# Chunked attention with memory keys, then a sine-activated two-layer network: x in two tiles, and the front of the first batch in another order

## The chip, the cores and the metric

The kernel runs on one core of one Trainium2 chip. A core has TensorE (PE) for matrix products, with its weight loads shown apart (PEld), VectorE (DVE), ScalarE (ACT), GpSimd (POOL) and SyncE (SP), and 16 DMA engines. POOL and SP have queues from which DMAs are issued. The metric is the device time of one execution, in microseconds.

## The reference

There are 4 batches of 768 tokens with 8 heads of 64. Tokens attend in chunks of 32: each chunk to 16 tokens before it, itself, 8 after it, and 8 memory keys of the batch and head. The result, as 3072 rows of 512, goes through two layers of width 2048 with a sine activation.

```python
for c in range(nc):                      # 24 chunks of 32 tokens
    q_c = q[:, :, c_start:c_end]
    k_full = np.concatenate([mem_k, k[:, :, l_start:r_end]], axis=2)
    v_full = np.concatenate([mem_v, v[:, :, l_start:r_end]], axis=2)
    a = softmax(q_c @ k_full.T / sqrt(64))
    out[:, :, c_start:c_end] = a @ v_full
x = out.transpose(0, 2, 1, 3).reshape(3072, 512)
h = x @ w_in
s = np.sin(alpha * h)
g = h + s * s / alpha
return g @ w_out
```

## The kernel before

**Stages.** The four batches go one after the other. For each there is attention, which leaves x transposed in a tile `xT` (128 partitions x 4 groups of features `kt` x 768 tokens, bf16), then the first layer (`layer`, lines 692 to 712): 16 blocks `ft` of 128 hidden features, for each of which `first` runs four matmuls over `kt` for each half of 384 tokens (`half_first`, line 508), then a sine on ACT (line 518), a square on ACT, DVE or POOL as a letter of the string `squares` says (lines 544 and 547), and a combination on DVE, `snake` (line 551), which writes the bf16 tile `gT`. The second layer (`second`, line 566 is its matmul) is a generator that `feed.take(n)` runs n matmuls of; a finished piece of 128 rows is copied out of PSUM by `end_o` (line 579 on DVE, line 581 on ACT) and sent by SP. So the second layer of one batch runs in pieces between the attention steps of the next batch and between its blocks.

**Order.** The program is scheduled by hand: each engine works in the order in which the code issues, and waits only for the data and the buffers of an instruction. The eight PSUM banks are handed out from rings (`plan`, `take_bank`); a ring is a written list, and a bank comes free when its last reader is done. `two` takes a bank and the one behind it, `single` one of the banks 6 and 7.

**Batch 0.** `attention_first` (line 390) works by pairs of heads `hp` and by halves of the tokens. `turn_k`, `turn_q` transpose keys and queries on PE; `sc_half` makes scores (lines 341 and 349 on PE) and exponentials (line 356 on ACT); `pv` makes the values (line 368 on PE, lines 374 and 375 on DVE); `x` transposes one block on PE (line 385) and copies it to `xT` (line 388, on ACT unless told otherwise). `warm(n)` issues n matmuls on zeros (line 336) into the bank at the head of the ring of `single`. In before the order from the third `pv` unit on is (1,0), (1,1), (2,0), (2,1), (3,0), (3,1). After the block (3,0), `ahead(0)` runs the first token half of layer block 0, and after (3,1) `ahead(1)` that of block 1; each has its sine and its square on ACT.

**Loads.** POOL issues the loads: keys and queries of batch 0 by pairs, v of batch 0 in parts (heads 0 and 1, then 2 and 3, 4 and 5, 6 and 7; each in two copies for two ranges of partitions), w_in in five, w_out in two, then memory values, keys and queries of batch 1, and the memory keys of batches 2 and 3 in two copies (line 685). The timeline of POOL shows the later of these waiting for the landing of earlier ones. POOL's squares of the first layer are behind them in its program.

**Later batches.** `attention` (line 473) works by 8 steps of 96 tokens. The first five blocks of x are transposed by SP's DMA transpose (line 492), the last three by PE and a DVE copy (line 329). `shares` says how many second-layer matmuls go into each step. Near the end, `ahead(0)`, `ahead(1)` and `ahead(2)` run the first token halves of three layer blocks. While `state["attending"]` holds, `end_o` copies on DVE.

Of the kernel before, what the change touches and what calls it, by code (L numbers as in the profile page):

```python
# [9 lines left out]
P = 128  # L10
QW = 96
# [31 lines left out]
def kernel(  # L43
# [76 lines left out]
    memk_st = consts.tile([P, 2, H * D], BF, name="memk_st")  # L120
# [17 lines left out]
    def load_rows(b):  # L138
        for jt in order:
# [18 lines left out]
            kst[64:72], memk_st[64:72, b - 2, :].unsqueeze(1).to_broadcast([NM, NJ, H * D])  # L158
# [117 lines left out]
    state = {"n": 0, "attending": False}  # L276
# [45 lines left out]

    def turn_x(xT, j, x_blk):
# [5 lines left out]
        nc.vector.tensor_copy(xT[:, :, QW * j:QW * j + QW], xtp)  # L329
# [52 lines left out]
    def unit_turn(xT, hp, half, x_blk, copy):  # L382
# [5 lines left out]
        copy(xT[:, hp, HALF * half:HALF * half + HALF].rearrange("p (j c) -> p j c", j=4), xtp)  # L388

    def attention_first(kq, alphas, ahead):  # L390
        xT = xp.tile([P, KT, S], BF, name="xT")
# [60 lines left out]
        pv(1, 1)  # L452
        sc_half(3, 1)
        x(1, 0)
        pv(2, 0)
        warm(1)
        x(1, 1)
        pv(2, 1)
        warm(2)
        x(2, 0)  # L460
        pv(3, 0)
        warm(2)
        x(2, 1)
        pv(3, 1)
        warm(1)
        x(3, 0)
        nc.scalar.preload_act_table(ACTF.Sin)
        ahead(0, 0, xT)
        x(3, 1, nc.vector.tensor_copy)
        ahead(1, 0, xT)  # L470
        return xT

    def attention(b, stream, shares, lag, crossed, beside=iter(()), beside_from=0):
        xT = xp.tile([P, KT, S], BF, name="xT")
        ptl, xbl = {}, {}
        state["attending"] = True
        for s in range(NJ + lag + 1):
# [8 lines left out]
            j = s - lag  # L486
            if j == NJ:
                ahead(1, 0, xT)
            if 0 <= j < NJ:
                xbl[j] = values(b, j, ptl.pop(j))  # L490
                if j < crossed:
                    nc.sync.dma_start_transpose(
                        xT[:, :, QW * j:QW * j + QW], xbl.pop(j)[:].rearrange("p g e d -> p (g e d)")
                    )
            stream.take(n - n // 2)
            if j == NJ - 1:
                ahead(0, 0, xT)
            if crossed <= j - 1 < NJ:
                turn_x(xT, j - 1, xbl.pop(j - 1))
        ahead(2, 0, xT)  # L500
        state["attending"] = False
# [4 lines left out]
    def half_first(hT, ft, hf, xT):  # L506
        for kt in range(KT):
            nc.tensor.matmul(  # L508
                hT[:, hf, 0:HALF],
                w_in_sb[:, kt, P * ft:P * ft + P],  # L510
                xT[:, kt, HALF * hf:HALF * hf + HALF],
# [5 lines left out]
    def sine(u, hT, ft, e):  # L517
        nc.scalar.activation(u[:, e], hT[:, e, 0:HALF], ACTF.Sin, scale=alpha_sb[:, ft:ft + 1])  # L518

    def ahead(ft, hf, xT):  # L520
        if ft < 3:
            hT = two("big")
            half_first(hT, ft, hf, xT)
            u = mlp.tile([P, 2, HALF], F32, name="u", bufs=4)
            e = slice(hf, hf + 1)
            sine(u, hT, ft, e)
            nc.scalar.activation(u[:, e], u[:, e], ACTF.Square)
            begun[ft] = (hT, u)

    def first(ft, xT, square, started=None):  # L530
        e = slice(0, 2)
# [280 lines left out]
```

## Time and profile before

| | us |
|---|---|
| median of 4 runs | 219.99 |
| lowest and highest of them | 218.99, 220.24 |
| the profiled execution | 219.91 |
| its span, first to last instruction | 218.1 |
| PE busy in it | 210.2 (96%) |
| ACT busy | 153.1 (70%) |
| DVE busy | 137.5 (63%) |
| POOL busy | 82.1 (38%) |

A row of the timeline gives the start in us from the first instruction, the length, the engine, the line, the operation, what is written from what, the shapes and the number of instructions that the row joins; in brackets stand the idle time of the engine before it and what ended that. A busy PE is not PE at its peak, since the ends of matmuls are modelled; what counts is the distance from start to start. The chain of waits follows the last instruction back to the first. A row of the busy times by stage gives the stage, its length, and for each engine the busy time and the number of instructions, then the granted TensorE clock and the DMA engines' share and rate. A row of the DMA issues gives the size of one and the time from issue to landing.

### The profile page before, as it was taken

Reading aid. Unit: us, or ns where it says so; the run is one execution under the profiler, and the core shown is the slowest. Engines: PE = TensorE matmul, PEld = TensorE weight load, DVE = VectorE, ACT = ScalarE, POOL = GpSimd, SP = SyncE. Lnnn points to the kernel's source line nnn. Section 1 sums busy time; section 2 is a strip of 40 time slices with the busy share of each in tenths; the row PEclk is TensorE's granted clock in tenths of the full one; section 3 lists DMA queues with packets and bytes.
Section 4 is the critical chain, followed back from the end, with each engine's and each line's share of the span. In section 5 each row is a group of like instructions: output and inputs, shape, how many; then the busy total and the mean of one; then the engine's idle time right before and its main releaser. Section 6 shows DMA issues by size and latency. Waiting matters only on the chain.

```text
span 218.1 us, 4457 instructions
## 1 busy us (share of the span) xinstructions
PE 210.2 (96%) x1687; PEld 114.2 (52%) x1687; DVE 137.5 (63%) x246; ACT 153.1 (70%) x238; POOL 82.1 (38%) x102
## 2 busy tenths in 40 slices
PE   7999998999999999999999999999999999999993
PEld 2555664555545555544555555545555555544453
DVE  5866659884527889995775766575854753871110
ACT  2457797895778899998967777988776778651010
POOL 7996663598700599500078099100000000000000
PEclk9999999999999999999999999999999999999999
DMA  5999999999999599999449999995330110111212
GB/s 76 160 171 168 206 209 206 200 193 122 112 193 187 56 155 147 164 165 124 99 62 174 112 111 150 191 218 150 68 103 2 48 51 2 48 48 51 96 48 96
DMA packets 98877, 26.96 MB, mean 124 GB/s; under 512 B 86808, under 2 KB 95912, under 8 KB 98856
## 3 DMA queue, kind: packets, MB, share of 16 engines
q0 software_dynamic: 71520, 14.82, 92.5%
q1 hardware_dynamic: 27336, 11.86, 26.3%
q8 instruction: 13, 0.21, 0.4%
q14 instruction: 8, 0.07, 0.1%
HBM read 29.69 MB, written 6.29 MB: 165 GB/s over the span
## 4 chain that ended last, share of the span: by engine, by line
PE 73%; DMA 10%; POOL 5%; DVE 5%; ACT 3%; issue 3%; DVEq 0%; ACTq 0%; POOLq 0%
PE ps L566 35%; PE ps L508 30%; DMA w_in_sb<-in_moe_w_in_dram 5%; DMA vw<-in_v_dram 4%; PE ps L283 3%; PE ps L309 2%; ACT u L518 2%; DVE gT L551 2%; DMA xT<-x_blk 2%; PE ps L589 2%; POOL vw L183 1%; POOL u L547 1%; POOL q_bf L172 1%; POOL k_bf L172 1%; PE ps L244 1%
## 5 line engine op out<-in xcount | busy, mean ns | idle before, releaser
L566 PE MATMUL ps<-w_out_sb,gT 128*128 128x512 bf16 x368 | 95.5, 380 | 0.2
L508 PE MATMUL ps<-xT,w_in_sb 128*128 128x384 bf16 x512 | 90.8, 326 | 1.9 <-DMA xT<-x_blk 0.8
L551 DVE SCALAR_TENSOR_TENSOR gT<-u,inv_alpha,ps 128x768 bf16<-128x768 f32 (+1 forms) x75 | 65.7, 895 | 23.4 <-ACT u L544 16.2
L518 ACT ACTIVATE u<-ps,alpha_sb 128x768 f32<-128x768 f32 (+1 forms) x75 | 59.4, 801 | 20.7 <-PE ps L508 20.1
L508 PEld LDWEIGHTS <-w_in_sb 128*128 128x128 bf16 x512 | 49.6, 98 | 39.0 <-issue 3.5
L566 PEld LDWEIGHTS <-gT 128*128 128x128 bf16 x368 | 32.8, 98 | 29.1 <-issue 0.5
L544 ACT ACTIVATE u<-u 128x768 f32<-128x768 f32 (+1 forms) x40 | 31.5, 787 | 1.2
L296 ACT ACTIVATE pt<-ps,biasm 128x256 bf16<-128x256 f32 x72 | 28.7, 472 | 4.6 <-PE ps L283 1.8
L579 DVE COPY o_sb<-ps 128x512 f32<-128x512 f32 x17 | 11.7, 689 | 27.3 <-PE ps L566 27.2
L183 POOL DMA_DIRECT2D vw<-in_v_dram x15 | 18.2, 1219 | 0.3 <-issue 0.3
L547 DVE TENSOR_TENSOR u<-u 128x768 f32<-128x768 f32 (+1 forms) x18 | 16.0, 886 | 1.7 <-ACT u L518 1.6
L316 DVE TENSOR_TENSOR x_blk<-ps,rinv 96x512 bf16<-96x512 f32 x24 | 16.5, 687 | 0.8
L143 POOL DMA_DIRECT2D kst<-in_k_dram x16 | 11.1, 694 | 5.8 <-DMA vw<-in_v_dram 5.2
L262 ACT COPY kT<-ps 128x672 bf16<-128x672 bf16 x8 | 5.7, 718 | 9.7 <-PE ps L247 7.3
L581 ACT COPY o_sb<-ps 128x512 f32<-128x512 f32 x6 | 3.5, 584 | 12.7 <-PE ps L566 12.7
L148 POOL DMA_DIRECT2D kst<-in_k_dram x16 | 11.7, 728 | 0.3 <-issue 0.2
L336 PE MATMUL ps<-idle 128*128 128x512 bf16 x30 | 10.4, 459 | 1.3 <-DVE vw L628 1.2
L309 PEld LDWEIGHTS <-pt 128*128 128x128 bf16 x192 | 9.0, 98 | 4.1
L153 POOL DMA_DIRECT2D qst<-in_q_dram x12 | 10.8, 901 | 1.0 <-DMA vw<-in_v_dram 1.0
L547 POOL TENSOR_TENSOR u<-u 128x768 f32<-128x768 f32 (+1 forms) x6 | 8.3, 1396 | 5.9 <-ACT u L518 5.9
L283 PEld LDWEIGHTS <-kT 64*128 64x128 bf16 x192 | 4.9, 94 | 10.4 <-issue 9.9
L315 DVE RECIPROCAL rinv<-ps 96x8 f32<-96x8 f32 x24 | 4.8, 202 | 8.2 <-ACT pt L296 5.2
(83 smaller groups left out, 146.0 us busy)
## 6 DMA issues: line engine op xcount, KB each, us to landing
out_dram<-o_sb SPq DMA_DIRECT2D x23, 256.0 KB
w_out_sb<-in_moe_w_out_dram POOLq DMA_DIRECT2D x2, 1024.0 KB, 18.0
w_in_sb<-in_moe_w_in_dram POOLq DMA_DIRECT2D x3, 512.0 KB, 10.5
vw<-in_v_dram POOLq DMA_DIRECT2D x3, 512.0 KB, 9.1
qst<-in_q_dram POOLq DMA_DIRECT2D x12, 128.0 KB, 5.9
vw<-in_v_dram POOLq DMA_DIRECT2D x2, 448.0 KB, 12.6
kst<-in_k_dram POOLq DMA_DIRECT2D x14, 64.0 KB, 5.6
kst<-in_k_dram POOLq DMA_DIRECT2D x14, 56.0 KB, 5.3
```

What stands on the lines that cost most here:

```text
L148: nc.gpsimd.dma_start(kst[72:72 + n, j, :].rearrange("p (h d) -> p h d", d=D), k[b, :, QW * j + 48:QW * j + 48 + n, :].rearrange("h p d -> ...
L183: nc.gpsimd.dma_start(vw[p0:p1, c0:c1, 0:D], flat[r0:r0 + QW * (c1 - c0)].rearrange("(n t) d -> t n d", t=QW)[0:p1 - p0],)
L296: nc.scalar.activation(pt[:, 0:H * QW].rearrange("p (g e c) -> p g e c", g=2, e=4)[:, :, :, 32 * m:32 * m + 32], sc[:, :, 0:4 * QW].rearra ...
L309: nc.tensor.matmul(otv[:, e, hp, :], pt[:, QW * i:QW * i + P], vws[b % 2][:, 2 * hp + e, j, 0:D + 1],)
L316: nc.vector.tensor_tensor(out=x_blk[:].rearrange("p g e d -> p e g d"), in0=otv[0:QW, :, :, 0:D], in1=rinv[:].unsqueeze(3).to_broadcast([Q ...
L508: nc.tensor.matmul(hT[:, hf, 0:HALF], w_in_sb[:, kt, P * ft:P * ft + P], xT[:, kt, HALF * hf:HALF * hf + HALF], start=(kt == 0), stop=(kt ...
L518: nc.scalar.activation(u[:, e], hT[:, e, 0:HALF], ACTF.Sin, scale=alpha_sb[:, ft:ft + 1])
L544: nc.scalar.activation(u[:, e], u[:, e], ACTF.Square)
L547: eng.tensor_tensor(out=u[:, e], in0=u[:, e], in1=u[:, e], op=ALU.mult)
L551: nc.vector.scalar_tensor_tensor(out=gT[:, ft, :].rearrange("p (e c) -> p e c", e=2)[:, e], in0=u[:, e], scalar=inv_alpha[:, ft:ft + 1], i ...
L566: nc.tensor.matmul(ps[:, bank, :], gT[:, ft, P * s:P * s + P], w_out_sb[:, ft, :], start=(ft == 0), stop=(ft == FT - 1),)
L579: nc.vector.tensor_copy(o_sb[:], ps[:, bank, :])
```

## The change

`xT` becomes a list of two tiles, one for each half of the tokens; `alloc_x` makes them and `block_of` finds the place of a block of 96. In `attention_first` the first halves of pairs 2 and 3 go before the second halves of pairs 1 to 3; two fewer fillers are issued after the third unit; three layer blocks instead of two have their first token half in the front, placed between the second-half blocks, with banks that are named; their sines come at the end, and their squares go to POOL, DVE and POOL instead of ACT. The loads of w_out, memory values, keys and queries of batch 1 (`next_loads`) are issued within the front. The two loads of memory keys are gone: `load_rows` sends the rows from `memk_bf`, which the front fills for all batches. The letters of batch 0's squares and the ring of its layer are new. In batch 1's attention the last second-layer matmul comes one step earlier, and from the step on that makes the values of the last block, `end_o` copies on ACT (`state["copying"]`). The sines of `ahead` move to `half_sine`, which in later batches follows at once, as before.

```diff
--- before.py
+++ after.py
@@ -117,7 +117,6 @@
     memv_st = consts.tile([P, B, H, D], BF, name="memv_st")
     kst = consts.tile([P, NJ, H * D], BF, name="kst")
     qst = consts.tile([P, NSUB, H * D], BF, name="qst")
-    memk_st = consts.tile([P, 2, H * D], BF, name="memk_st")
     memkT = consts.tile([P, HP, 32], BF, name="memkT")
     w_in_sb = consts.tile([P, KT, d_ff], BF, name="w_in_sb")
     w_out_sb = consts.tile([P, FT, d_model], BF, name="w_out_sb")
@@ -155,7 +154,9 @@
                     q[b, :, P * t:P * t + P, :].rearrange("h p d -> p h d"),
                 )
         nc.sync.dma_start(
-            kst[64:72], memk_st[64:72, b - 2, :].unsqueeze(1).to_broadcast([NM, NJ, H * D])
+            kst[64:72],
+            memk_bf[NM * b:NM * b + NM].rearrange("n h d -> n (h d)").unsqueeze(1)
+            .to_broadcast([NM, NJ, H * D]),
         )
 
     def cross_steps(b):
@@ -273,7 +274,7 @@
 
 
 
-    state = {"n": 0, "attending": False}
+    state = {"n": 0, "attending": False, "copying": False}
 
     def scores(b, j, kind="big"):
         pitch = 104 if b < 2 else P
@@ -320,13 +321,20 @@
         )
         return x_blk
 
+    def alloc_x():
+        return [xp.tile([P, KT, HALF], BF, name=f"xT{hf}") for hf in range(2)]
+
+    def block_of(xT, j):
+        c = QW * (j % 4)
+        return xT[j // 4][:, :, c:c + QW]
+
     def turn_x(xT, j, x_blk):
         xtp = packed(single(), KT, QW)
         for kt in range(KT):
             nc.tensor.transpose(
                 xtp[:, kt, :], x_blk[:, kt].rearrange("p e d -> p (e d)"), ident[0:QW, 0:QW]
             )
-        nc.vector.tensor_copy(xT[:, :, QW * j:QW * j + QW], xtp)
+        nc.vector.tensor_copy(block_of(xT, j), xtp)
 
 
 
@@ -385,10 +393,10 @@
             nc.tensor.transpose(
                 xtp[:, jj, :], x_blk[:, jj].rearrange("p e d -> p (e d)"), ident[0:QW, 0:QW]
             )
-        copy(xT[:, hp, HALF * half:HALF * half + HALF].rearrange("p (j c) -> p j c", j=4), xtp)
-
-    def attention_first(kq, alphas, ahead):
-        xT = xp.tile([P, KT, S], BF, name="xT")
+        copy(xT[half][:, hp, :].rearrange("p (j c) -> p j c", j=4), xtp)
+
+    def attention_first(kq, alphas, ahead, next_loads):
+        xT = alloc_x()
         pt, xb = {}, {}
 
         def turn_k(hp):
@@ -449,29 +457,34 @@
         plan(big=(4, 0, 2))
         pv(1, 0)
         sc_half(3, 0)
-        pv(1, 1)
+        pv(2, 0)
         sc_half(3, 1)
         x(1, 0)
-        pv(2, 0)
         warm(1)
-        x(1, 1)
-        pv(2, 1)
+        pv(3, 0)
+        x(2, 0)
+        warm(1)
+        pv(1, 1)
+        next_loads()
         warm(2)
-        x(2, 0)
-        pv(3, 0)
-        warm(2)
-        x(2, 1)
-        pv(3, 1)
-        warm(1)
         x(3, 0)
         nc.scalar.preload_act_table(ACTF.Sin)
-        ahead(0, 0, xT)
+        plan(big=(0, 2))
+        pv(2, 1)
+        ahead(0, xT, (4, 1))
+        x(1, 1)
+        pv(3, 1)
+        ahead(1, xT, (5, 2))
+        x(2, 1)
+        ahead(2, xT, (0, 3))
+        plan(big=(4, 0, 2))
         x(3, 1, nc.vector.tensor_copy)
-        ahead(1, 0, xT)
+        for ft in range(3):
+            half_sine(ft, "PVP"[ft])
         return xT
 
     def attention(b, stream, shares, lag, crossed, beside=iter(()), beside_from=0):
-        xT = xp.tile([P, KT, S], BF, name="xT")
+        xT = alloc_x()
         ptl, xbl = {}, {}
         state["attending"] = True
         for s in range(NJ + lag + 1):
@@ -484,73 +497,88 @@
             if s >= beside_from:
                 next(beside, None)
             j = s - lag
+            state["copying"] = j >= NJ - 1
             if j == NJ:
-                ahead(1, 0, xT)
+                ahead(1, xT)
+                half_sine(1)
             if 0 <= j < NJ:
                 xbl[j] = values(b, j, ptl.pop(j))
                 if j < crossed:
                     nc.sync.dma_start_transpose(
-                        xT[:, :, QW * j:QW * j + QW], xbl.pop(j)[:].rearrange("p g e d -> p (g e d)")
+                        block_of(xT, j), xbl.pop(j)[:].rearrange("p g e d -> p (g e d)")
                     )
             stream.take(n - n // 2)
             if j == NJ - 1:
-                ahead(0, 0, xT)
+                ahead(0, xT)
+                half_sine(0)
             if crossed <= j - 1 < NJ:
                 turn_x(xT, j - 1, xbl.pop(j - 1))
-        ahead(2, 0, xT)
-        state["attending"] = False
+        ahead(2, xT)
+        half_sine(2)
+        state["attending"] = state["copying"] = False
         return xT
 
 
 
-    def half_first(hT, ft, hf, xT):
+    def half_first(bank, ft, hf, xT):
         for kt in range(KT):
             nc.tensor.matmul(
-                hT[:, hf, 0:HALF],
+                ps[:, bank, 0:HALF],
                 w_in_sb[:, kt, P * ft:P * ft + P],
-                xT[:, kt, HALF * hf:HALF * hf + HALF],
+                xT[hf][:, kt, :],
                 start=(kt == 0), stop=(kt == KT - 1),
             )
 
     begun = {}
 
     def sine(u, hT, ft, e):
-        nc.scalar.activation(u[:, e], hT[:, e, 0:HALF], ACTF.Sin, scale=alpha_sb[:, ft:ft + 1])
-
-    def ahead(ft, hf, xT):
-        if ft < 3:
-            hT = two("big")
-            half_first(hT, ft, hf, xT)
-            u = mlp.tile([P, 2, HALF], F32, name="u", bufs=4)
-            e = slice(hf, hf + 1)
-            sine(u, hT, ft, e)
-            nc.scalar.activation(u[:, e], u[:, e], ACTF.Square)
-            begun[ft] = (hT, u)
+        nc.scalar.activation(u[:, e], hT, ACTF.Sin, scale=alpha_sb[:, ft:ft + 1])
+
+    def ahead(ft, xT, banks=None):
+        if banks is None:
+            bank = take_bank("big")
+            banks = (bank, bank + 1)
+        half_first(banks[0], ft, 0, xT)
+        begun[ft] = (banks, mlp.tile([P, 2, HALF], F32, name="u", bufs=4))
+
+    def square_on(kind, x):
+        if kind == "A":
+            nc.scalar.activation(x, x, ACTF.Square)
+        else:
+            eng = nc.vector if kind == "V" else nc.gpsimd
+            eng.tensor_tensor(out=x, in0=x, in1=x, op=ALU.mult)
+
+    def half_sine(ft, square="A"):
+        banks, u = begun[ft]
+        e = slice(0, 1)
+        sine(u, ps[:, banks[0]:banks[0] + 1, 0:HALF], ft, e)
+        square_on(square, u[:, e])
+
+    def half_snake(gT, ft):
+        banks, u = begun[ft]
+        snake(gT, ft, ps[:, banks[0]:banks[0] + 1, 0:HALF], u, slice(0, 1))
 
     def first(ft, xT, square, started=None):
-        e = slice(0, 2)
         if started is not None:
-            hT, u = started
+            (_, bank), u = started
             e = slice(1, 2)
         else:
-            hT = two("h")
-            half_first(hT, ft, 0, xT)
+            bank = take_bank("h")
+            half_first(bank, ft, 0, xT)
             u = mlp.tile([P, 2, HALF], F32, name="u", bufs=4)
-        half_first(hT, ft, 1, xT)
+            e = slice(0, 2)
+        half_first(bank + (started is None), ft, 1, xT)
+        hT = ps[:, bank:bank + (2 if started is None else 1), 0:HALF]
         sine(u, hT, ft, e)
 
         def squared():
-            if square == "A":
-                nc.scalar.activation(u[:, e], u[:, e], ACTF.Square)
-            else:
-                eng = nc.vector if square == "V" else nc.gpsimd
-                eng.tensor_tensor(out=u[:, e], in0=u[:, e], in1=u[:, e], op=ALU.mult)
+            square_on(square, u[:, e])
         return hT, u, e, squared
 
     def snake(gT, ft, hT, u, e):
         nc.vector.scalar_tensor_tensor(
             out=gT[:, ft, :].rearrange("p (e c) -> p e c", e=2)[:, e],
-            in0=u[:, e], scalar=inv_alpha[:, ft:ft + 1], in1=hT[:, e, 0:HALF],
+            in0=u[:, e], scalar=inv_alpha[:, ft:ft + 1], in1=hT,
             op0=ALU.mult, op1=ALU.add,
         )
 
@@ -575,7 +603,7 @@
             rings["one"].remove(bank)
             rings["one"].append(bank)
             o_sb = mlp.tile([P, d_model], F32, name="o_sb", bufs=2)
-            if s % 2 == 0 or state["attending"]:
+            if (s % 2 == 0 or state["attending"]) and not state["copying"]:
                 nc.vector.tensor_copy(o_sb[:], ps[:, bank, :])
             else:
                 nc.scalar.copy(o_sb[:], ps[:, bank, :])
@@ -673,17 +701,17 @@
         nc.vector.tensor_copy(alpha_sb[:], at)
         nc.vector.reciprocal(inv_alpha[:], alpha_sb[:])
 
+    def next_loads():
+        for c in range(2):
+            load_w_out(c)
+        nc.gpsimd.dma_start(memv_st[64:72, 1:B].rearrange("n b h d -> n (b h) d"),
+                            mem_v[1:B].rearrange("b h n d -> n (b h) d"))
+        kq1.extend(alloc_qk())
+        load_qk(1, kq1, 0, H)
+
     feed = Feed()
-    xT = attention_first(kq, alphas, ahead)
-    for c in range(2):
-        load_w_out(c)
-    nc.gpsimd.dma_start(memv_st[64:72, 1:B].rearrange("n b h d -> n (b h) d"),
-                        mem_v[1:B].rearrange("b h n d -> n (b h) d"))
-    kq1 = alloc_qk()
-    load_qk(1, kq1, 0, H)
-    for bb in range(2):
-        nc.gpsimd.dma_start(memk_st[64:72].rearrange("n b (h d) -> n b h d", d=D)[:, bb],
-                            mem_k[2 + bb].rearrange("h n d -> n h d"))
+    kq1 = []
+    xT = attention_first(kq, alphas, ahead, next_loads)
 
 
 
@@ -694,7 +722,7 @@
         pend = []
         fed = 0
         for ft in sorted(begun):
-            snake(gT, ft, *begun[ft], slice(0, 1))
+            half_snake(gT, ft)
         for ft in range(FT):
             begin(ft)
             square = squares[ft % len(squares)]
@@ -714,8 +742,8 @@
     prs = []
 
     def begin_0(ft):
-        if ft == 2:
-            plan(h=[rings["big"][0], 6] + rings["big"][1:])
+        if ft == 3:
+            plan(h=[6] + rings["big"])
         if ft == 12:
             load_v(1)
             send_memv(1)
@@ -723,7 +751,7 @@
         if ft == 15:
             prs.extend(pair_up(kq1[n // HP], n % HP) for n in range(4))
 
-    layer(0, xT, "VPPAPAVPAVPPAAAA", begin_0, 0)
+    layer(0, xT, "PPPAVPPAAVPAAAAA", begin_0, 0)
     last4 = rings["h"]
     plan(one=(last4[0], last4[0] + 1), t=(last4[1], last4[1] + 1), big=last4[1:])
     put_memk(1)
@@ -742,7 +770,7 @@
     nc.scalar.preload_act_table(ACTF.Exp)
     load_v(2)
     feed.take(4)
-    xT = attention(1, feed, (6, 8, 4, 4, 4, 3, 3, 3, 3, 1, 1), 2, 5)
+    xT = attention(1, feed, (6, 8, 4, 4, 4, 3, 3, 3, 3, 2), 2, 5)
 
     for i in range(1, B):
         last = i == B - 1
@@ -750,13 +778,13 @@
 
         def begin(ft, i=i):
             if i == 1 and ft == 0:
-                nc.gpsimd.tensor_copy(gate[:], xT[0:1, 0, QW * 6 - 1:QW * 6])
+                nc.gpsimd.tensor_copy(gate[:], block_of(xT, 5)[0:1, 0, QW - 1:QW])
                 load_rows(2)
                 for _ in crossings:
                     pass
             if i == 2:
                 if ft == 0:
-                    nc.gpsimd.tensor_copy(gate[:], xT[0:1, 0, QW * 6 - 1:QW * 6])
+                    nc.gpsimd.tensor_copy(gate[:], block_of(xT, 5)[0:1, 0, QW - 1:QW])
                     load_v(3)
                     load_rows(3)
                 if ft >= 1:
```

## The prediction

> **What bounds the kernel now.** I read the page's parts 1 and 5 first, then the busy time by stage, then the front on PE, POOL and the DMA issues, then the places where PE is idle later.
>
> ```profile
> PE 210.2 (96%) x1687; PEld 114.2 (52%) x1687; DVE 137.5 (63%) x246; ACT 153.1 (70%) x238; POOL 82.1 (38%) x102
> L508 PE MATMUL ps<-xT,w_in_sb 128*128 128x384 bf16 x512 | 90.8, 326 | 1.9 <-DMA xT<-x_blk 0.8
> 25.60:47.10 21.50, 20.71 (x129) 12.28 (x128) 16.17 (x20) 19.12 (x25) 12.29 (x11) 1.00 1.28 205
> 75.80:96.40 20.60, 20.52 (x122) 11.79 (x121) 18.98 (x24) 19.87 (x28) 13.92 (x19) 1.00 2.04 157
> ```
>
> The windows' columns are PE, PEld, DVE, ACT, POOL. PE sets the time: only PE idleness or PE filler can be won. In the two stages of pure first-layer work (batch 0, then batch 1) ACT and DVE are at 19 to 20 of 20.6 to 21.5 us as well, so a PE that arrives earlier there soon waits for them.
>
> ```profile
> 18.97 0.40 PE L368 MATMUL ps<-vw,pt_first 128*128 128x65 bf16 x8 [0.25 <-DMA vw<-in_v_dram]
> 21.26 0.41 PE L368 MATMUL ps<-vw,pt_first 128*128 128x65 bf16 x8
> 23.02 0.41 PE L368 MATMUL ps<-vw,pt_first 128*128 128x65 bf16 x8
> 24.53 0.34 PE L385 MATMUL ps<-ident,x_blk 96*128 96x96 bf16 x4
> 24.71 1.05 PE L508 MATMUL ps<-xT,w_in_sb 128*128 128x384 bf16 x4
> 25.77 7.32 PE L508 MATMUL ps<-xT,w_in_sb 128*128 128x384 bf16 x44
> 33.87 13.39 PE L508 MATMUL ps<-xT,w_in_sb 128*128 128x384 bf16 x80 [0.79 <-DVE gT L551]
> ...
> vw<-in_v_dram POOLq DMA_DIRECT2D x1, 112.0 KB, 7.9
> vw<-in_v_dram POOLq DMA_DIRECT2D x1, 112.0 KB, 7.5
> ...
> 29.92 0.58 POOL L685 DMA_DIRECT2D memk_st<-in_mem_k_dram  x1 [1.97 <-DMA w_in_sb<-in_moe_w_in_dram]
> 30.51 2.26 POOL L547 TENSOR_TENSOR u<-u 128x384 f32<-128x384 f32 x2
> ```
>
> The L368 rows are the values of pairs 1, 2 and 3, first halves; L508 is the first layer. From 25.77 PE runs at full rate (44 matmuls, 0.163 us from start to start) until a bank waits at 33.08 for an L551 (the snake), which waits for a POOL square, which waits behind the memory-key loads: POOL stood 1.97 us for a free place in its queue. The two vw lines are DMA issues in windows around 13.5 and 15.3: second parts of v for heads 4, 5 (issued 13.17) and 6, 7 (issued 14.85). They land at 13.17 + 7.9 = 21.05 and 14.85 + 7.5 = 22.38.
>
> ```profile
> 74.77 0.69 DVE L579 COPY o_sb<-ps 128x512 f32<-128x512 f32 x1 [0.51 <-PE ps L566]
> 75.78 19.24 PE L508 MATMUL ps<-xT,w_in_sb 128*128 128x384 bf16 x116 [0.22 <-DVE xT L329]
> 154.50 3.88 DMA xT<-x_blk
> 158.51 0.81 PE L508 MATMUL ps<-xT,w_in_sb 128*128 128x384 bf16 x4 [0.82 <-DMA xT<-x_blk]
> ```
>
> Two later PE waits touch the change: batch 1's last x copy queued behind an output copy on DVE, and batch 3's wait for an x transpose.
>
> **The two x tiles: nothing.** At 24.71 the half layer starts before the last first-half x copy on ACT (24.91 to 25.39) and before any copy of x(3,1), so waits already go by region. In batch 3 the chain says that PE waited for the transpose issued at 154.50, the fourth. The fifth, the first of the second half, is issued from 157.48 to 158.70, after PE had started. The fourth is needed with two tiles too: that wait stays. Its bounds: 0.8 gained if its timing shifts by luck, nothing lost; I take 0.
>
> **The new order of the front.** Gaps measured in before: values to reciprocal 0.44, reciprocal to block ready 0.93, scores to exponential 0.80, turning to its ACT copy 0.38. On PE: values 0.25, half scores 0.70, turning 0.17, filler 0.215, half layer 0.65.
> - values(2,0) moves from 21.26 to 19.91, but its v lands at 21.05: PE idles to 21.17 (values(1,0), too, went about 0.1 after its landing). Queued behind it: half scores (3,1), 21.42, whose exponential ends at 23.0 instead of 22.0, and on ACT behind that the copy of x(1,0), to about 23.4.
> - values(3,0) goes at 22.5, right at its landing. The second filler writes the bank of x(1,0) and waits for that copy: 23.46, another 0.5 idle. values(1,1) 23.67, two fillers, x(3,0) at 24.35 (before 24.53).
> - ahead(0) 24.77 to 25.42, then x(1,1), values(3,1), ahead(1), x(2,1), ahead(2), x(3,1) without a pause, 0.17 + 0.25 + 0.65 + 0.17 + 0.65 + 0.17 = 2.07, to 27.49. The DVE copy of x(3,1) ends at 28.11, and the 16th layer matmul at 28.33.
> - next_loads moves ahead of ten pieces of the front. On POOL its five issues (w_out twice, memory values, k, q; 21.32 to 26.04) pass nothing, since POOL has no other work in the front, and each waits for a place in the queue as before: landings unchanged, 0. SP issues nothing there. The two key issues that went behind them (1.17 us, with 1.31 and 1.97 of waiting) are gone.
>
> 16 matmuls at 28.33 equal full rate from 28.33 - 16 x 0.163 = 25.73. Before, 4 at 25.77 equal 25.12. Two fillers fewer and one more half layer in the front thus end as a loss of 0.6, because v is late. ACT, too, starts its sines later, 27.4 against 26.70: two x copies stand behind the table load.
>
> **Batch 0's layer.** From 25.12, 128 matmuls at 0.1626 would end at 45.93; they end at 47.10, so waits cost 1.17, of which the one at 33 is 0.95 (start to start 1.11 instead of 0.16). Without the key loads POOL is free at 26.04, not 30.50. I replayed the layer engine by engine with the durations above, snake 0.97 (half 0.55), sine 0.93 (0.58), square on ACT 0.75, DVE 0.95 (0.55), POOL 1.47 (0.84); for before it gives 47.02. With the new squares and bank order no bank is late up to ft 12; at ft 13 one is late by 0.24 (ft 9's square on DVE). It ends at 46.76, or 46.54 without that wait: a gain of 0.26 to 0.56, I take 0.35. A rule speaks against the moved squares: the Trainium skill, GPSIMD Engine Reference, 4.1 Engine selection, puts two-input elementwise work on VectorE, GpSimd being about twice as slow. The trace has 839 ns against 551 (half), 1466 against 951: 1.5 times. By the rule the five halves that POOL now takes first are 5.5 us instead of 4.2, the square of ft 2 comes 1.3 later, and PE waits 0.8 at ft 6: the gain is gone. I take the row.
> What comes next covers the rest: ACT ends its squares at 49.9 either way and is idle 2.0 before the k copies; q lands 26.1 after its issue, at 51.25, and its first use is at 52.04, so 0.35 of earlier PE is covered, 1 us would not be. v of batch 1 (used from 63.7) is issued some 1.7 us earlier.
>
> **Batch 1.** The last output piece moves ahead of the half layer: it fills a 0.15 wait before 72.88. Its copy goes to ACT (0.58) where ACT idles 0.76; the last x copy is no longer late: 0.39 (start to start 0.55 at 75.23). So PE is 0.54 earlier. But the sines begin no earlier (73.8 against 73.73), the bank of ft 0 is free at 78.8 and PE wants it at 78.5: 0.34 goes back. Net 0.15; ends 0 and 0.54. In batches 2 and 3 an output copy of 0.58 on ACT delays the sines by about 0.4; the bank it delays was free 0.67 early in batch 2 (snake to 116.64, PE at 117.31) and 1.3 in batch 3 (164.68, 166.00): 0. If that cover were gone, 0.4 each.
> **Memory keys by SP from memk_bf:** the same issue on SP (0.72 at 75.92), from a tile filled at 5.6: 0.
>
> Sum: 219.91 (the profiled execution: span 218.1 and 1.8 around it; 0.08 below the median of 219.99) - 0.35 - 0.15 = 219.4.
>
> **The rivals.** (A, 0.50) The sum, 218.7 to 220.2. (B, 0.26) Faster: the filler's wait or the v landing costs less, layer 1 keeps all of the 0.54, and batch 3's transpose comes in time: 0.56 + 0.54 + 0.8 = 1.9, 218.0. For it: each is a real PE wait of before. Against: ACT and DVE are nearly full in both layers. (C, 0.24) Slower: the front now leaves PE 1.8 us idle between 19.9 and 23.5, with two fillers fewer, and the array falls to its half rate. The first ten fillers of before step 0.427 us, later ones 0.216: a slow state of about 4 us. PE has no slack from 23.5 to 28.3, so about 2 us: 219.4 + 2.0 = 221.4. It decides from the step after 21.2: 0.427 or 0.216. Against it: after the 0.79 idle at 33 the steps stay at 0.163, with PEclk 1.00. The Trainium skill, TensorE: Matmul & The Clock Gate, Part 1, asks an idle window of some 3.4 us; my pause is broken up by scores and values. No row here has such a mixture, so it keeps a chance. (D) That the two tiles do nothing is already in the sum.
>
> **How the numbers follow.** 0.5% is 1.1 us, about what a measurement of this kernel can tell from no change. Of A a quarter lies beyond it (0.12): faster 0.12 + 0.26 = 0.38, same 0.38, slower 0.24. The range goes from B to C: 217.9 to 221.3; A's own is 218.7 to 220.2.
>
> **What would show it.** Right: a PE wait of about 1.2 on v before the values of pair 2; the last x copy of the front at 28, not 26; sines from 27.4; no wait on L551 near 33; L508 of batch 0 ending near 46.7; no L329 wait before batch 1's layer, but one on L551 early in it; the 0.8 transpose wait still in batch 3. Wrong: L508 of batch 0 ending before 46 or after 47.3, half-rate steps in the front, or the transpose wait gone.

## The result, and the profile after

The kernel with the change took 218.95 us in the median (44 runs, 217.85 to 220.24), the kernel before 219.82 us (63 runs, 218.57 to 221.22): ratio 0.9964, 95% interval 0.9952 to 0.9976. By the ratio that is 0.79 us less, between 0.53 and 1.06 (0.87 between the two medians), inside the likeliest case of the prediction and a little faster than its 219.4.

The profiled execution of after has the same span as that of before, 218.1 us (219.86 us in all). It shows no gain because its first loads landed later: values(1,0), the start of the part that was changed, runs at 19.60, in before at 18.97. So the two traces are compared from that point on, and a time in after is to be read as 0.63 us less when it is set beside one in before.

The lines of the page, then of the busy times by stage, that answer to those shown of before (columns of the latter PE, PEld, DVE, ACT, POOL, granted clock, DMA); the stages here are the unbroken runs of first-layer matmuls, 116 of them in batch 0 against 124 in before's window, so their lengths can't be compared:

```profile
PE 210.3 (96%) x1685; PEld 114.3 (52%) x1685; DVE 136.3 (63%) x244; ACT 154.1 (71%) x241; POOL 81.2 (37%) x102
L525 PE MATMUL ps<-xT,w_in_sb 128*128 128x384 bf16 x512 | 90.8, 326 | 1.1 <-DMA xT<-x_blk 0.8
```

```profile
27.70:46.90 19.20, 19.10 (x120) 11.33 (x118) 16.25 (x21) 17.21 (x24) 12.33 (x11) 1.00 1.28 204
74.60:94.50 19.90, 19.77 (x123) 11.68 (x121) 18.00 (x24) 19.55 (x28) 15.16 (x20) 1.00 1.85 151
```

L525 is the first layer's matmul (L508 before). Its idle time fell from 1.9 to 1.1 us, and of what is left 0.8 is the transpose wait of batch 3, which the change doesn't touch. PE is now busy in 19.10 of 19.20 us of batch 0's layer.

The timeline of the front, for PE, then ACT, DVE and POOL (L376 values, L344 fillers, L535 sines, L396 the copy of a turned block, L549 squares):

```profile
19.60 0.40 PE L376 MATMUL ps<-vw,pt_first 128*128 128x65 bf16 x8 [0.21 <-DMA vw<-in_v_dram]
...
21.40 0.40 PE L376 MATMUL ps<-vw,pt_first 128*128 128x65 bf16 x8 [0.80 <-DMA vw<-in_v_dram]
...
23.67 0.38 PE L344 MATMUL ps<-idle 128*128 128x512 bf16 x1 [0.23 <-ACT xT L396]
...
24.98 0.81 PE L525 MATMUL ps<-xT,w_in_sb 128*128 128x384 bf16 x4
...
27.69 19.43 PE L525 MATMUL ps<-xT,w_in_sb 128*128 128x384 bf16 x116
46.96 0.59 PE L594 MATMUL ps<-w_out_sb,gT 128*128 128x512 bf16 x2
...
27.47 1.54 ACT L535 ACTIVATE u<-ps,alpha_sb 128x384 f32<-128x384 f32 x3
27.96 0.36 DVE L396 COPY xT<-ps 128x384 bf16<-128x384 bf16 x1 [0.77 <-PE ps L393]
28.15 4.28 POOL L549 TENSOR_TENSOR u<-u 128x384 f32<-128x384 f32 x5 [2.19 <-ACT u L535]
```

The wait for v that the prediction put at 1.2 us is there with 0.80, and the second filler behind it waits 0.23 for a copy. Then one row of 116 matmuls runs to the second layer: where before had a row of 44, a hole of 0.79 and a row of 80, after has no hole of that size. From start to start it has two short waits, 0.19 ahead of the matmul at 28.37, whose x the DVE copy of x(3,1) ends at 28.32, and 0.23 ahead of the one at 43.06, for a bank. POOL's five half squares start as soon as the first sine is done; in before POOL was still busy with the memory-key loads until 30.5.

Batch 1 and batch 2, on PE and ACT (L609 is the output copy on ACT, L334 the turning of the last blocks of x):

```profile
73.00 0.59 ACT L609 COPY o_sb<-ps 128x512 f32<-128x512 f32 x1 [0.18 <-PE ps L594]
73.76 0.58 ACT L535 ACTIVATE u<-ps,alpha_sb 128x384 f32<-128x384 f32 x1 [0.17 <-PE ps L525]
...
74.56 19.98 PE L525 MATMUL ps<-xT,w_in_sb 128*128 128x384 bf16 x120
...
111.90 0.57 ACT L609 COPY o_sb<-ps 128x512 f32<-128x512 f32 x1
111.91 0.59 PE L594 MATMUL ps<-w_out_sb,gT 128*128 128x512 bf16 x2
112.52 0.33 PE L334 MATMUL ps<-ident,x_blk 96*128 96x96 bf16 x4
```

In batch 1 the output copy fits on ACT ahead of the first sine, and PE enters the layer without the wait for DVE. In batch 2 two L594 matmuls start at 111.91 and step 0.216 us; L334 could follow at 112.34, and follows at 112.52, just after ACT's output copy (111.90 to 112.47) gives back the bank that it writes. That is a loss of 0.18 us that the prediction didn't have.

The chain of waits in batch 3, and the row at its end:

```profile
154.10 4.02 DMA xT<-x_blk
158.12 0.14 issue
158.25 0.81 PE ps L525 x4
```

```profile
158.25 0.81 PE L525 MATMUL ps<-xT,w_in_sb 128*128 128x384 bf16 x4 [0.84 <-DMA xT<-x_blk]
```

PE waits 0.84 us for the fourth transpose, as in before (0.82).

Start to start, from values(1,0) on (us; #n is the n-th first-layer matmul counted from 0, #16, #127 and so on):

| stretch | before | after | gain |
|---|---|---|---|
| values(1,0) to #16: front | 8.76 | 8.93 | -0.17 |
| #16 to #127: rest of batch 0's layer | 19.21 | 18.27 | 0.94 |
| #127 to #128: batch 1's attention | 25.94 | 26.11 | -0.17 |
| #128 to #255: batch 1's layer | 21.81 | 21.30 | 0.51 |
| #255 to #383 | 46.92 | 47.12 | -0.20 |
| #383 to #511 | 51.27 | 51.48 | -0.21 |

The sum is 0.70, close to the 0.79 of the timing. Each row compares one execution with one, and before's rows vary too: with the same code in batch 0's layer, #16 to #127 takes 19.21 in before, 19.00 in two_tiles and 18.93 in tail_only (both below). The eight traces that have the new squares on POOL and no key loads all take 18.3. So the layer gains between 0.7 and 0.9.

### The profile page after: what moved, and what is told of

Read it like the earlier page. It is cut to its first block, busy times and chain, and to the rows that moved or that the text cites. A ratio compares the mean times of both kernels' runs of the same rounds, so it can differ in the third digit from the quotient of the medians.

```text
span 218.1 us, 4454 instructions
## 1 busy us (share of the span) xinstructions
PE 210.3 (96%) x1685; PEld 114.3 (52%) x1685; DVE 136.3 (63%) x244; ACT 154.1 (71%) x241; POOL 81.2 (37%) x102
## 4 chain that ended last, share of the span: by engine, by line
PE 71%; DVE 7%; ACT 6%; DMA 6%; POOL 5%; issue 3%; DVEq 0%; ACTq 0%; POOLq 0%
PE ps L594 35%; PE ps L525 26%; ACT u L535 4%; DVE gT L579 4%; DMA vw<-in_v_dram 4%; PE ps L284 3%; POOL vw L184 2%; PE ps L310 2%; DVE u L549 2%; DMA xT<-x_blk 2%; PE ps L617 2%; ACT u L546 1%; POOL q_bf L173 1%; POOL k_bf L173 1%; PE ps L245 1%
## 5 line engine op out<-in xcount | busy, mean ns | idle before, releaser
L594 PE MATMUL ps<-w_out_sb,gT 128*128 128x512 bf16 x368 | 95.5, 380 | 0.2
L525 PE MATMUL ps<-xT,w_in_sb 128*128 128x384 bf16 x512 | 90.8, 326 | 1.1 <-DMA xT<-x_blk 0.8
L535 ACT ACTIVATE u<-ps,alpha_sb 128x768 f32<-128x768 f32 (+1 forms) x76 | 59.4, 796 | 19.0 <-PE ps L525 18.8
L525 PEld LDWEIGHTS <-w_in_sb 128*128 128x128 bf16 x512 | 49.4, 98 | 37.7 <-issue 2.4
L594 PEld LDWEIGHTS <-gT 128*128 128x128 bf16 x368 | 32.8, 97 | 29.1 <-issue 0.5
L546 ACT ACTIVATE u<-u 128x768 f32<-128x768 f32 (+1 forms) x50 | 37.0, 741 | 1.6
L607 DVE COPY o_sb<-ps 128x512 f32<-128x512 f32 x14 | 9.6, 689 | 26.7 <-PE ps L594 26.7
L549 DVE TENSOR_TENSOR u<-u 128x768 f32<-128x768 f32 (+1 forms) x18 | 16.2, 901 | 1.9 <-ACT u L535 1.9
L609 ACT COPY o_sb<-ps 128x512 f32<-128x512 f32 x9 | 5.2, 580 | 12.9 <-PE ps L594 12.9
L549 POOL TENSOR_TENSOR u<-u 128x384 f32<-128x384 f32 (+1 forms) x8 | 8.6, 1100 | 8.6 <-ACT u L535 8.5
L344 PE MATMUL ps<-idle 128*128 128x512 bf16 x28 | 10.2, 481 | 1.4 <-DVE vw L656 1.2
```

The costliest lines, as they stand in the source:

```text
L525: nc.tensor.matmul(ps[:, bank, 0:HALF], w_in_sb[:, kt, P * ft:P * ft + P], xT[hf][:, kt, :], start=(kt == 0), stop=(kt == KT - 1),)
L535: nc.scalar.activation(u[:, e], hT, ACTF.Sin, scale=alpha_sb[:, ft:ft + 1])
L546: nc.scalar.activation(x, x, ACTF.Square)
L549: eng.tensor_tensor(out=x, in0=x, in1=x, op=ALU.mult)
L594: nc.tensor.matmul(ps[:, bank, :], gT[:, ft, P * s:P * s + P], w_out_sb[:, ft, :], start=(ft == 0), stop=(ft == FT - 1),)
```

## The experiments

Each was timed against before in the same sitting; the ratio stands with its 95% interval.

**Memory keys off the queue, alone (keys_only) and put back (keys_back).** keys_only is before without the two POOL loads; keys_back is after with them.

```diff
-            kst[64:72], memk_st[64:72, b - 2, :].unsqueeze(1).to_broadcast([NM, NJ, H * D])
+            kst[64:72], memk_bf[NM * b:NM * b + NM].rearrange("n h d -> n (h d)")...
...
-    for bb in range(2):
-        nc.gpsimd.dma_start(memk_st[64:72]...[:, bb], mem_k[2 + bb]...)
```

> Before, with the memory keys sent from memk_bf and their two loads taken off the POOL queue; nothing else. Theory 1 (key loads and front only pay together): the wait at 33 turns into others, because the snakes that free the banks of ft 4, 6 and 10 hang on ACT and DVE too; the replay of the layer gives 46.91 against 47.02 for its end, so 0.0 to 0.2 us faster, ratio 0.999 to 1.000. Theory 2 (the key loads are the whole gain): the 0.95 wait vanishes without another in its place, 0.8 us faster, ratio 0.9964.

> After, with the two key loads back on the POOL queue behind the keys and queries of batch 1. Theory 1: five half squares now stand behind the loads on POOL, which is free only at about 30.5; the first bank is 1.5 us late at ft 4 and one more 0.4 late at ft 8: the layer ends 1.8 us later than in after, so 1.0 us slower than before, ratio 1.0045. Theory 2: exactly the gain is lost, ratio 1.000.

keys_only: 0.9995 (0.9977 to 1.0014), as theory 1 had it. keys_back: 1.0103 (1.0070 to 1.0136), some 3 us above after: slower than either theory. POOL, then PE in keys_back:

```profile
26.26 0.59 POOL L711 DMA_DIRECT2D memk_st<-in_mem_k_dram  x1 [1.54 <-DMA w_in_sb<-in_moe_w_in_dram]
28.81 0.58 POOL L711 DMA_DIRECT2D memk_st<-in_mem_k_dram  x1 [1.96 <-DMA w_in_sb<-in_moe_w_in_dram]
29.41 3.96 POOL L548 TENSOR_TENSOR u<-u 128x384 f32<-128x384 f32 x5
...
30.95 5.50 PE L524 MATMUL ps<-xT,w_in_sb 128*128 128x384 bf16 x32 [1.42 <-DVE gT L578]
38.17 2.11 PE L524 MATMUL ps<-xT,w_in_sb 128*128 128x384 bf16 x12 [1.73 <-DVE gT L578]
```

Two loads cost PE two waits of 1.4 and 1.7 us here, since the queue in which they wait for a place (1.54 and 1.96 us) is also the engine that squares. From start to start beyond the full rate the first is 1.59, near the 1.5 of theory 1, and the second, at ft 8, is 1.89 where theory 1 had 0.4: that is where it fell short. With the old order of squares (keys_only) the same removal buys nothing measurable: start to start, the wait at 33 shrinks from 0.95 to 0.31, and two others, 0.21 at 38.5 and 0.27 at 42.6, are there in the place of one of 0.16. The layer takes 18.90, about the 18.93 of tail_only, which still has the key loads. The removal and the new squares pay only together.

**Where the squares sit (squares_dve).** The kernel after with ft 0 to 2's first halves and the first three letters on DVE:

```diff
-            half_sine(ft, "PVP"[ft])
+            half_sine(ft, "VVV"[ft])
...
-    layer(0, xT, "PPPAVPPAAVPAAAAA", begin_0, 0)
+    layer(0, xT, "VVVAVPPAAVPAAAAA", begin_0, 0)
```

> After with the squares of ft 0, 1 and 2 on DVE, both halves, instead of POOL (ft 1's first half is there already). By the rule that elementwise work belongs on VectorE, a half square is 0.55 instead of 0.84 us: no slower than after, 0.9964 or less. Theory 1 (DVE is the fuller engine there, POOL's time is free): DVE gets 2.75 us more work ahead of the snakes that free the banks; the replay has banks late at ft 4, 5, 6 and 8, the layer ends 1.9 later than in after: 1.1 us slower than before, ratio 1.005.

1.0053 (1.0034 to 1.0072): about 2.0 us above after, as theory 1 had it. PE waits for the snake on DVE at 32.8, 34.0 and 35.6, by 0.54, 0.28 and 1.24 us beyond the full rate; the rows around the first and the last:

```profile
33.54 2.38 PE L525 MATMUL ps<-xT,w_in_sb 128*128 128x384 bf16 x12 [0.37 <-DVE gT L579]
36.99 3.25 PE L525 MATMUL ps<-xT,w_in_sb 128*128 128x384 bf16 x19 [1.07 <-DVE gT L579]
```

So the slower engine was the right one: a half square takes 0.86 us on POOL (28.15 4.28 x5 above) and 0.55 on DVE, but DVE has the snakes to do. Over batch 0's layer it is busy for 16.25 of 19.20 us in after (27.70:46.90) and for 18.14 of 20.20 in squares_dve (27.00:47.20), POOL for 12.33 and 8.38.

**Two tiles alone (two_tiles).** Before with `alloc_x` and `block_of`, all else as it was.

```diff
-        xT = xp.tile([P, KT, S], BF, name="xT")
+        xT = alloc_x()
...
```

> Before with x in two tiles and nothing else. Theory 1 (waits go by region already, the tiles do nothing): ratio 1.000 within 0.001. Rival (the half layer of the later batches waits for blocks of the other half, which two tiles end): the transpose wait of batch 3 and the one of batch 1 shrink, up to 0.8 us, ratio 0.9964.

1.0008 (0.9987 to 1.0028): nothing, and batch 3's wait is there (1.16 us).

**The tail of batch 1 (tail_only, copy_b1, front_only).** tail_only puts batch 1's shares and its output copies on ACT into before. copy_b1 keeps them in after, but only in batch 1. front_only takes the tail away from after in all batches.

```diff
-            state["copying"] = j >= NJ - 1
+            state["copying"] = b == 1 and j >= NJ - 1     # copy_b1, from after
```

> Before with the end of batch 1's attention as in after: the last second-layer matmul one step earlier and the output copy on ACT, in batch 1 alone. As predicted: PE 0.54 earlier into the layer, 0.34 given back at ft 4, ratio 0.9993. By the profile of after (PE is 0.40 earlier at the start of the layer and 0.34 at its end, against the stage before): ratio 0.9984. Rival: nothing passed on by a layer in which ACT and DVE are full, 1.000.

> After, with the output copies at the end of the attention on ACT in batch 1 only, on DVE in batches 2 and 3 as in before. Theory 1: the copy on ACT keeps a bank that the turning of the last x block needs, 0.18 us of PE in each of batches 2 and 3, so 0.4 us faster than after: 1.2 faster than before, ratio 0.9946. Rival: later waits take it up again (PE is covered there by second-layer work), ratio as after, 0.9964.

> The kernel after with the tail of every attention as before (copies of o_sb by turns on both engines, batch 1's shares 6 8 4 4 4 3 3 3 3 1 1): the new front, the two tiles and the keys off the queue are left. Theory 1 (stage sums of the traces): layer 0 keeps its gain of 0.77 at the start of the second layer, batch 1 loses its 0.34, batches 2 and 3 get their 0.18 each back: net 0.79, ratio about 0.9964. Rival (the tail carries the gain, as tail_only's 0.9972 alone would say): the front alone is worth under 0.3 us, ratio 0.9985 or more.

tail_only 0.9972 (0.9957 to 0.9988), copy_b1 0.9954 (0.9936 to 0.9971), front_only 0.9976 (0.9952 to 0.9999). tail_only gains 0.61 us (0.26 to 0.94), more than each of its three expectations had, though the interval reaches the second. From #128 to #255 tail_only and copy_b1 take 21.30 us like after, front_only 21.80 like before: the 0.51 belongs to the tail. In copy_b1 the waits of 0.18 before L334 in batches 2 and 3 are gone, which shows where they came from; its interval holds both its expectations, so the timing alone doesn't. DVE, then PE at the end of batch 2's attention:

```profile
109.57 0.69 DVE L607 COPY o_sb<-ps 128x512 f32<-128x512 f32 x1
110.02 0.59 PE L594 MATMUL ps<-w_out_sb,gT 128*128 128x512 bf16 x2
110.45 0.34 PE L334 MATMUL ps<-ident,x_blk 96*128 96x96 bf16 x4
```

The copy on DVE starts 0.45 us ahead of the two L594, where the copy on ACT started together with them.

front_only gains 0.53 us (0.02 to 1.06), an interval that holds both the 0.79 of theory 1 and its rival. Its trace has the gain of the first layer (27.00 from values(1,0) to the second layer, in before 28.13), and then loses 0.64 to a transpose wait ahead of batch 1's layer, where before has 0.15. The sum of tail_only and front_only (0.61 + 0.53) is 0.35 more than after gains, and after loses 0.41 in the stretches of batches 2 and 3; with intervals this wide the two figures can't be called the same thing.

**The order of the values (pv11_first, pv11_copy).** values(2,0) waits for v that lands late; values(1,1) needs only what is there. pv11_first puts it ahead; pv11_copy does it in copy_b1.

```diff
         sc_half(3, 0)
-        pv(2, 0)
+        pv(1, 1)
         sc_half(3, 1)
         x(1, 0)
+        pv(2, 0)
         warm(1)
         pv(3, 0)
         x(2, 0)
-        warm(1)
-        pv(1, 1)
         next_loads()
```

> After, with the values (1,1) before those of (2,0), in the gap in which PE waits for v of heads 4 and 5, and one filler fewer. Theory 1: PE comes to full rate 0.4 us earlier (replay of the front 25.31 instead of 25.72) and layer 0 passes most of it on: 0.2 to 0.4 faster than after, ratio 0.9946 to 0.9955. Rival: ACT and DVE set the end of layer 0 and nothing is passed on, ratio 0.9964.

> After with both: values (1,1) before those of (2,0), and the output copies on ACT in batch 1 only. The two sit in different batches, so the gains should add: 0.7 from the first and 0.2 to 0.4 from the second on top of the 0.8 of after, 1.7 to 1.9 us faster than before, ratio 0.9914 to 0.9922. Rival: the gain in the front is taken up by later waits once the batches behind it move too: 0.9931 as with the first alone.

pv11_first 0.9931 (0.9907 to 0.9954), pv11_copy 0.9919 (0.9891 to 0.9947). Both beat after, but not where I had expected, and that pv11_copy met its number is luck: values(1,0) to the second layer is 27.36 us in pv11_first, the same as in after, and 27.02 in pv11_copy against 26.79 in copy_b1, with v landing alike (1.11 and 1.09 us behind values(1,0)). What had gone was the wait ahead of batch 3, over 100 us later.

**Why batch 3's wait comes and goes (pv11_filler, after_less1, copy_less1).** Queue q8 of the page's part 3, called `instruction`, carries 13 packets of 16 KB in an execution, each of which takes 0.9 to 2.0 us. In each trace I set the start of the one that falls near batch 3's fourth transpose against the issue of that transpose:

| kernel | packet after the issue, us | PE idle ahead of batch 3's layer, us |
|---|---|---|
| two_tiles | 0.98 | 1.16 |
| tail_only | 1.23 | 0.99 |
| keys_back | 1.30 | 1.10 |
| before | 1.31 | 0.82 |
| copy_b1 | 1.81 | 0.51 |
| after | 1.86 | 0.84 |
| keys_only | 1.87 | 0.46 |
| squares_dve | 1.95 | 0.66 |
| pv11_first | 2.33 | 0 |
| pv11_copy | 3.52 | 0 |

pv11_first has one filler matmul fewer than after. The new theory, that the number of instructions and not the order had moved the packet, was tried with one filler more or fewer at the very start, where PE waits for the first loads anyway:

```diff
-    warm(11)
+    warm(12)      # pv11_filler, from pv11_first
...
-    warm(11)
+    warm(10)      # after_less1, from after; copy_less1, from copy_b1
```

> pv11_first with one filler matmul more at the very start of the kernel (12 for 11), so that TensorE's queue has as many instructions as in the kernel after. The filler's time is covered by the wait for the first loads. Theory 1 (instruction loads): where a load of instructions falls against the four transposes of batch 3 decides whether TensorE waits for them, and that is set by the number of instructions. With the number of the kernel after back, the wait of about 0.8 us ahead of batch 3's first matmul returns; ratio to before 0.996 to 0.998. Theory 2 (order): the wait went because values (1,1) ahead of (2,0) shifts the stages; it stays away, ratio 0.993 to 0.994.

> The kernel after with one filler matmul fewer at the very start (10 for 11); nothing else changes. Theory 1 (instruction loads): the count is now that of pv11_first, so the wait ahead of batch 3's first matmul (0.84 idle) goes, and the ratio to before is about 0.9925. Theory 2 (order): nothing changes, 0.996 to 0.997 with the wait of 0.8 still there.

> copy_b1 (the kernel after, o_sb copies kept on ScalarE only in batch 1) with one filler fewer at the start. Theory 1 (instruction loads): 0.9954 less about 0.5 us of wait ahead of batch 3, so 0.992 to 0.993, like pv11_copy. Theory 2 (order): 0.995 to 0.996, the wait ahead of batch 3 stays at 0.5 or more.

pv11_filler 0.9965 (0.9943 to 0.9987), after_less1 0.9921 (0.9892 to 0.9951), copy_less1 0.9903 (0.9869 to 0.9936), the fastest of all, at 217.92 us against 219.96. Theory 1 held in all three. Batch 3 in pv11_filler, then in after_less1, on PE:

```profile
158.32 0.81 PE L524 MATMUL ps<-xT,w_in_sb 128*128 128x384 bf16 x4 [1.25 <-DMA xT<-x_blk]
```

```profile
155.83 0.59 PE L594 MATMUL ps<-w_out_sb,gT 128*128 128x512 bf16 x2
156.26 0.81 PE L525 MATMUL ps<-xT,w_in_sb 128*128 128x384 bf16 x4
```

In the ten traces of the table PE waits where the packet starts within 2 us of the issue, and not where it starts 2.3 us or more behind it. The four later traces agree: in pv11_filler the packet starts 1.40 after the issue and PE idles 1.25, in front_only 1.81 and 0.92, in after_less1 and copy_less1 3.69 and 3.98 and PE doesn't idle there at all.

The traces also hold every DMA packet, and these show how the transpose is held up. From 1.1 to 2.1 us behind the issue of the fourth transpose its queue (q1) runs 416 packets: 384 of 256 bytes and 32 of 4 bytes. This is so in pv11_first (154.70 to 155.70) and in after_less1 (154.38 to 155.38):

```profile
q1 hardware_dynamic: 416, 0.10, 49.8%
```

```profile
q1 hardware_dynamic: 416, 0.10, 50.0%
```

In pv11_filler the same microsecond (154.95 to 155.95) has 390 of them and a packet of q8, and the other 26 come in the window 156.65 to 157.55, right behind that packet, which ends at 156.81:

```profile
q1 hardware_dynamic: 390, 0.09, 46.2%
q8 instruction: 1, 0.02, 9.7%
```

```profile
q1 hardware_dynamic: 26, 0.01, 6.8%
```

26 is a sixteenth of 416, the share of one of the 16 DMA engines if they share the transpose evenly. So I read it that this engine finishes the instruction packet before it goes on with the transpose. In after (155.20 to 156.20) the packet comes later and only the last two packets, of 4 bytes, are behind it:

```profile
q1 hardware_dynamic: 414, 0.10, 49.7%
q8 instruction: 1, 0.02, 6.6%
```

All ten traces with the wait are of one of these two kinds: 26 or 2 packets follow the instruction packet, beginning within 20 ns of its end. All four without it have their 416 packets done by 2.03 us. PE starts 0.8 to 1.2 us behind the last of the late packets.

Shown by timing is that one filler more or fewer moves the time: by 0.75 us from pv11_first to pv11_filler (whose intervals overlap), 0.95 from after to after_less1 (0.9951 against 0.9952 where they come closest) and 1.1 from copy_b1 to copy_less1 (which meet at 0.9936), each time the way that was expected. In the traces of after and after_less1 the stretch #383 to #511 falls from 51.48 to 50.48, and no other stretch changes by more than 0.14. Open is why a filler moves the packet as far as it does, up to 2.2 us (copy_b1 to copy_less1), and how much its place varies between executions: each kernel has one trace. Before with one filler fewer was not run, so how much of such a gain it would have without the change is not known. Waits for a transpose stand ahead of batch 1's or batch 2's layer in some traces too (0.64 in front_only, 0.46 in keys_only); they were not followed up.

## Why the prediction was right

**What it had right.** The places of the waits: one on v before the values of pair 2, none near 33, one late bank at ft 13 with 0.24 (0.23 measured), the DVE wait before batch 1's layer gone, two tiles worth nothing (two_tiles), and the transpose wait still there. The mechanism of batch 0's layer is confirmed from both sides: keys_only without the new squares, and squares_dve and keys_back without one of the two, all lack the gain. The rule of the Trainium skill, GPSIMD Engine Reference, 4.1 Engine selection, that two-input elementwise work belongs on VectorE, was followed in squares_dve and cost 2.0 us: it prices one instruction, and in this layer the sum on each engine decides. The half rate of rival C is absent: the two fillers at 24.13 step 0.216 us, and the granted clock is 1.00 from 18 to 25.

**What fitted by luck.** The sines of the front from 27.4 (27.47) and the last x copy at 28 (27.96) agree as they stand, but after's execution runs 0.63 us late from the first loads on. From values(1,0) on, the sines come 0.56 us sooner than predicted.

**The front, predicted as a loss of 0.6.** The step that was too large is "its v lands at 21.05: PE idles to 21.17". That was a landing of one execution, 2.07 us behind values(1,0). In the fourteen traces it lies between 1.02 and 2.07, and before's is the latest of them. In after it is 1.66, the wait 0.80 and the loss 0.17. The seven traces that have after's order of the front show how much hangs on it:

| v behind values(1,0), us | 1.02 | 1.06 | 1.09 | 1.19 | 1.31 | 1.53 | 1.66 |
|---|---|---|---|---|---|---|---|
| values(1,0) to #16, us | 8.31 | 8.33 | 8.36 | 8.46 | 8.58 | 8.79 | 8.93 |

The front lasts as much longer as v lands later. The four traces with the old order take 8.75 or 8.76 with landings from 1.09 to 2.07, since their values of pair 2 start only 2.29 behind values(1,0) (before). The new front gains 0.18 to 0.45 us in five of the seven and loses up to 0.17 in the other two. Carried on to a landing of 2.07 the row gives an estimate of 9.34, a loss of 0.58. The replay of the front was right, and its one input was the extreme one.

**Batch 0's layer.** The trace gives 0.94 from #16 on, for which the prediction had 1.17 of waits less the one of 0.24 that stays; with the small loss in front the net is 0.77, where it took 0.35. One reading was wrong: DVE is busy for 16.17 of the 21.50 us of batch 0's stage in before, not 19 to 20; only ACT is (19.12).

**Batch 1.** "The bank of ft 0 is free at 78.8 and PE wants it at 78.5: 0.34 goes back" failed: nothing goes back there; the row of 120 matmuls from 74.56 shows no hole where the prediction put one. By the code, ft 4 needs the late bank only for its second half, four matmuls or 0.65 us after its first; that reading was not tried by itself. The 0.51 gained less the 0.17 lost in the attention before it gives 0.34, not 0.15. Not all of the 0.17 is the matmul moved ahead: with the same tail that stretch takes 26.00 to 26.02 in copy_b1, pv11_copy and copy_less1, 26.11 in after and 25.94 in before.

**Batches 2 and 3, predicted as nothing.** The prediction weighed only the banks of the sines. The copy on ACT also holds the bank in which the last block of x is turned: 0.18 in each, 0.2 with the rest of the stretch, shown by copy_b1.

**Batch 3's transpose wait.** "0.8 gained if its timing shifts by luck" was about right in size (1.0 from after to after_less1) and left open what the luck was: where a packet of the instruction queue falls, which a filler matmul at the start of the program moves.

So the sum of 0.50 met a measured 0.79 with terms that were off by 0.4 (front), 0.2 (batch 1) and -0.4 (batches 2 and 3) in the pair of traces; that they nearly cancel is no merit of the working.

## What to carry to other kernels

When an engine both issues loads and computes, a small load at the end of its queue is priced by the wait for its place and by what computes behind it, and its removal pays only if the work is laid on the engine that it frees. Before moving an output copy to another engine, list every reader and writer of its bank, not just the next big user. And when a transfer is late by a microsecond without a cause in the code, look at the instruction queue in the trace, and shift the program by one harmless instruction before explaining the difference by the edit under test. A stall worked out from one landing wants the landing of several executions.

## What the runs showed of the hardware

- A packet of the instruction queue (16 KB, 0.9 to 2.0 us) held up a DMA transpose: where it began 1.0 to 1.95 us behind the transpose's issue, the last 26 or 2 of the transpose's 416 packets ran only when it had ended, and PE idled 0.46 to 1.25 us. That is so in ten traces of ten; in the four with the packet 2.3 us or more behind, PE didn't idle.
- One filler matmul more or fewer at the start of the program moved such a packet by 0.9 to 2.2 us against the transpose, and the time by about as much as the whole change, 0.75 to 1.1 us.
- The same load of v landed between 1.02 and 2.07 us behind the same point of the program, over fourteen traces; a stall computed from one landing carries that spread.
- Two small loads at the end of GpSimd's queue waited 1.54 and 1.96 us for a place in it, and the squares behind them waited with them: 3 us of the kernel's time (keys_back).
